# Taking the GpSimd relay out from between two convolution fills, and cutting the last store in three

## The chip, the cores and the metric

The kernel runs on one core of one Trainium2 chip. The metric is device microseconds of one execution. Beside it stands the span in the profile, from the first to the last instruction; in nearly every run here the time is 1.8 us above the span.

## The reference, cut to what matters

A causal convolution of width 7 per head over the sequence (8 heads of 24 channels, softmax-normalised weights), then a gated feed-forward layer.

```python
# x (8, 4096, 192); weight (8, 7); w_gate, w_val (192, 1536); w_out (1536, 192)
w    = softmax(weight, axis=-1)
conv = sum_k w[h, k] * x_padded[:, t + k, h]           # 32768 rows of 192
g    = conv @ w_gate
out  = (g * sigmoid(g) * (conv @ w_val)) @ w_out
```

## The kernel before

Rows are worked in 64 blocks of 512; two blocks (index `a` = 0 and 1) make a unit. TensorE convolves a unit with Toeplitz matrices in two *fills* of four heads. The result is evicted from PSUM into `stage`, transposed into `xq`, and goes through the gate, value and output matmuls. Unit 0 is transposed on TensorE; from unit 1 on `stage` goes through DRAM and comes back by three DMA transposes per block. Matmuls have 64 rows, so two run side by side as row tiles.

When two row tiles swap the PSUM banks that they write, the kernel puts in a *relay*: a GpSimd no-op that waits for the last matmul so far, and that the next such matmul waits for. The Trainium skill ("TensorEngine Tiling (Array Packing)", Gotcha 1: PSUM Pressure) gives the reason: row tiles cannot access the same PSUM bank at once, and software has to see to it. No run here tests that hazard.

```python
    def after_relay(mm):                     # called for conv and w_out matmuls
        last_mm[0] = mm
        if relay[0] is not None:
            tc.add_manual_dep(mm.ins, relay[0].ins.name, SYNC, ...)
            relay[0] = None

    def emit_relay():
        relay[0] = nc.gpsimd.nop(nofuse=True)
        tc.add_manual_dep(relay[0].ins, last_mm[0].ins.name, SYNC, ...)
    ...
    # head, in program order (cut)
    while first: emit_fetch(first)           # x of unit 0, GpSimd queue
    emit_busy(14)                            # filler matmuls that keep TensorE busy
    emit_gv_load(0); emit_gv_load(1); emit_wo_load(0); emit_gv_load(2)   # GpSimd queue
    ...                                      # Toeplitz matrices
    emit_busy(6)
    for fill in range(2):
        emit_conv(0, fill, spare=(fill == 1))      # fill 0 -> cps banks, fill 1 -> gate/val banks
        emit_relay()
        for a, mul in enumerate((nc.scalar.mul, nc.vector.tensor_scalar_mul)):
            emit_conv_out(0, fill, a, mul)         # ScalarE evicts block a=0, VectorE a=1
        if fill == 0:
            emit_dup(0, nc.vector.tensor_copy)
    first = fetches(1)                             # x of unit 1
    while first: emit_fetch(first)
    emit_wo_load(1)
    emit_busy(6)
    for b in range(UB):
        emit_pe_transpose_out(b, emit_pe_transpose(b))   # reads conv[0][rows, b, ...]
    emit_busy(4)
    # main loop: u is the unit, s the step in it; unit 1's conv at u = 0, s = 7 and 10,
    # DMA transposes of block 2 at s = 12..14; in between (cut):
            f0 = 14 if u == 0 else 0               # when unit u+2's x is loaded
    # last block's store
        if b == n_blocks - 1:
            nc.scalar.dma_start(out=o_v[:, 0:2], in_=o_sb[:, 0:2])
            return lambda: nc.sync.dma_start(out=o_v[:, 2:4], in_=o_sb[:, 2:4])
```

## Time and profile before

| | before |
|---|---|
| time, median of the first 3 runs | 813.46 us (812.72 to 813.50) |
| profiled run: time, span | 812.60, 810.8 us |
| TensorE busy | 802.2 us, 99% of the span |
| fill 0 / fill 1 of unit 0 begin | 8.66 / 10.49 us |
| first gate matmul | 13.73 us |
| last eviction ends, end of span | 807.05, 810.8 us |

From the profile's page (engine, busy us, share of the span and instructions; then the chain of waits by engine, POOL being GpSimd):

```profile
span 810.8 us, 30886 instructions
PE 802.2 (99%) x12884; PEld 507.5 (63%) x12884; DVE 558.5 (69%) x866; ACT 554.1 (68%) x967; POOL 133.6 (16%) x195
...
PE 98%; POOL 1%; issue 0%; DVE 0%; POOLq 0%
```

TensorE is the bound nearly everywhere. The 1% of GpSimd sits in the head. The chain of waits there, in order of time (start, us, what):

```profile
8.38 0.84 POOL wo_sb L145
9.22 0.62 POOL w_sb L139
9.83 0.60 POOL w_sb L140
10.44 0.01 POOLq L255
10.45 0.04 issue
10.49 0.24 PE gate L288
```

Fill 1 (`gate L288`) waited for the relay (L255), and the relay for GpSimd's issuing of weight loads, 0.6 to 0.84 us each. The same place in the timeline (start, us, engine, line, operation, output<-input; in brackets the idle time before it and what ended it; `cps`, `gate` and `val` are PSUM tiles):

```profile
9.32 0.57 ACT L304 ACTIVATE stage<-cps_198 128x480 f16<-128x480 f32 x1 [1.23 <-PE cps_199 L288]
9.36 0.66 DVE L304 TENSOR_SCALAR stage<-cps_199 128x480 f16<-128x480 f32 x1 [1.27 <-PE cps_199 L288]
10.12 0.47 DVE L312 COPY stage<-stage 128x640 f16<-128x640 f16 x1
10.49 0.24 PE L288 MATMUL gate<-x_0_82,toep 58*64 58x120 f16 x1 [1.21 <-POOLq L255]
11.14 0.57 ACT L304 ACTIVATE stage<-gate 128x480 f16<-128x480 f32 x1 [1.25 <-PE val L288]
11.18 0.66 DVE L304 TENSOR_SCALAR stage<-val 128x480 f16<-128x480 f32 x1 [0.59 <-PE val L288]
12.12 0.20 PE L346 MATMUL gate<-identity,stage 52*128 52x52 f16 x1
```

The reader is to see ScalarE (ACT), VectorE (DVE), and the transposes (L346). The tail, and below it the share and rate of the DMA engines in 40 slices of 0.11 us from 806.5 us on:

```profile
806.32 0.48 ACT L426 COPY o_sb<-acc_19289 128x384 f32<-128x384 f32 x1 [1.98 <-PE acc_19289 L414]
806.49 0.56 DVE L427 COPY o_sb<-acc_19290 128x384 f32<-128x384 f32 x1 [0.83 <-PE acc_19290 L414]
806.83 0.41 ACTq L430 DMA_DIRECT2D out_dram<-o_sb  x1
807.07 0.42 SPq L431 DMA_DIRECT2D out_dram<-o_sb  x1
```

```profile
DMA  0000000000059999999998400000000000000000
GB/s 0 0 0 0 0 0 0 0 0 0 0 123 294 375 348 321 314 308 328 328 328 301 130 0 0 0 0 0 0 0 0 0 0 0 0 0 0 0 0 0
```

Data moves for 1.3 us near 325 GB/s, then nothing for 1.9 us. For a DMA that GpSimd issues, the Trainium skill ("DMA: Bandwidth & Descriptors", Anatomy of one DMA) puts most of a fixed cost of about 2 us down to the receipt of the last write, heaviest for HBM. This store goes over the hardware queues of SP and ScalarE, which that section does not measure; the 1.9 us are of the same size.

### The profile page before, as it was taken

What the parts mean: (1) busy time and instruction counts of PE and PEld (TensorE: products, weight loads), DVE (VectorE), ACT (ScalarE), POOL (GpSimd) and SP (SyncE); (2) the same over time, 40 slices, a digit from 0 to 9 for tenths busy, and PEclk for the clock granted to TensorE, in tenths of its full rate; (3) what the DMA queues carried; (4) which work ended last, traced back from release to release, by engine and by line L of the source; (5) the groups of instructions that cost most, each with busy time, mean ns of one, the idle gap of its engine ahead of it and who ended that gap; (6) DMA issues with size and microseconds to landing.
All of it is one profiled execution on the core that took longest, in us unless ns stands there. A gap on an engine that the chain in (4) does not pass through costs nothing.

```text
span 810.8 us, 30886 instructions
## 1 busy us (share of the span) xinstructions
PE 802.2 (99%) x12884; PEld 507.5 (63%) x12884; DVE 558.5 (69%) x866; ACT 554.1 (68%) x967; POOL 133.6 (16%) x195
## 2 busy tenths in 40 slices
PE   7999999999999999999999999999999999999997
PEld 4666666666666666666666666666666666666665
DVE  6666667766667666677666767666776667676675
ACT  5677676667676776766777767767667677677664
POOL 6111111121111111111111111112111121111100
PEclk9999999999999999999999999999999999999999
DMA  9595654556554755546555556555555655464321
GB/s 136 94 143 99 117 96 97 124 97 112 117 90 108 131 98 110 95 99 122 110 109 108 84 115 130 99 104 105 99 119 104 119 104 92 107 130 92 92 75 40
DMA packets 187770, 85.53 MB, mean 105 GB/s; under 512 B 147678, under 2 KB 182590, under 8 KB 187630
## 3 DMA queue, kind: packets, MB, share of 16 engines
q0 software_dynamic: 52048, 42.26, 30.1%
q1 hardware_dynamic: 135310, 41.11, 24.3%
q8 instruction: 100, 1.64, 0.8%
q14 instruction: 40, 0.33, 0.1%
q10 hardware_dynamic: 272, 0.20, 0.1%
HBM read 34.95 MB, written 41.67 MB: 94 GB/s over the span
## 4 chain that ended last, share of the span: by engine, by line
PE 98%; POOL 1%; issue 0%; DVE 0%; POOLq 0%
PE gate L370 61%; PE val L370 1%; PE acc_763 L398 0%; PE acc_421 L398 0%; PE acc_420 L398 0%; PE acc_1702 L398 0%; PE acc_1363 L398 0%; PE acc_16113 L398 0%; PE acc_6505 L398 0%; PE acc_17314 L398 0%; PE acc_14912 L398 0%; PE acc_14575 L398 0%; PE acc_11310 L398 0%; PE acc_10971 L398 0%; PE acc_9772 L398 0%; PE acc_7706 L398 0%
## 5 line engine op out<-in xcount | busy, mean ns | idle before, releaser
L385 DVE TENSOR_TENSOR h<-sig,val 128x512 f16<-128x512 f16 x768 | 520.5, 688 | 242.8 <-PE val L370 240.9
L380 ACT ACTIVATE sig<-gate 128x512 f16<-128x512 f32 x768 | 458.5, 597 | 242.6 <-PE val L370 212.6
L370 PE MATMUL val<-xq,w_sb 64*128 64x512 f16 x2304 | 590.2, 376 | 0.0
L370 PE MATMUL gate<-xq,w_sb 64*128 64x512 f16 x2304 | 589.8, 376 | 0.0
L398 PEld LDWEIGHTS <-h 64*128 64x128 f16 x6120 | 268.2, 94 | 120.3
L370 PEld LDWEIGHTS <-w_sb 64*128 64x128 f16 x4608 | 212.7, 94 | 143.9 <-issue 1.2
L432 POOL DMA_DIRECT2D out_dram<-o_sb x63 | 48.5, 770 | 414.0 <-PE val L370 376.2
L288 PEld LDWEIGHTS <-toep 58*64 58x64 f16 x2048 | 29.4, 106 | 28.0 <-POOLq L255 14.1
L113 POOL DMA_DIRECT2D x_1_83<-in_x_dram x33 | 23.9, 724 | 94.2 <-PE val L370 79.7
L113 POOL DMA_DIRECT2D x_0_82<-in_x_dram x40 | 28.3, 709 | 61.9 <-PE val L370 49.5
L312 POOL COPY stage<-stage 128x640 f16<-128x640 f16 x31 | 22.3, 720 | 50.0 <-ACT sig L380 48.6
L98 POOL MEMSET x_0_82<- 6x192 f16 x8 | 2.0, 247 | 39.7 <-PE acc_8569 L398 6.1
L156 PE MATMUL busy<-idle 128*128 128x384 f16 x30 | 7.0, 386 | 0.0
L398 PE MATMUL acc_2301<-wo_sb,h 64*128 64x192 f16 x48 | 5.2, 243 | 0.0
L398 PE MATMUL acc_4104<-wo_sb,h 64*128 64x192 f16 x48 | 5.2, 243 | 0.0
L398 PE MATMUL acc_4968<-wo_sb,h 64*128 64x192 f16 x48 | 5.2, 243 | 0.0
L398 PE MATMUL acc_7706<-wo_sb,h 64*128 64x192 f16 x48 | 5.2, 243 | 0.0
L398 PE MATMUL acc_8570<-wo_sb,h 64*128 64x192 f16 x48 | 5.2, 243 | 0.0
L398 PE MATMUL acc_13712<-wo_sb,h 64*128 64x192 f16 x48 | 5.2, 243 | 0.0
L398 PE MATMUL acc_14576<-wo_sb,h 64*128 64x192 f16 x48 | 5.2, 243 | 0.0
L398 PE MATMUL acc_17314<-wo_sb,h 64*128 64x192 f16 x48 | 5.2, 243 | 0.0
L398 PE MATMUL acc_18180<-wo_sb,h 64*128 64x192 f16 x48 | 5.2, 243 | 0.0
(564 smaller groups left out, 871.3 us busy)
## 6 DMA issues: line engine op xcount, KB each, us to landing
out_dram<-o_sb POOLq DMA_DIRECT2D x63, 384.0 KB, 3.5
x_1_83<-in_x_dram POOLq DMA_DIRECT2D x31, 240.0 KB, 5.0
x_0_82<-in_x_dram POOLq DMA_DIRECT2D x24, 240.0 KB, 4.7
x_0_82<-in_x_dram POOLq DMA_DIRECT2D x8, 216.0 KB, 3.9
w_sb<-in_moe_w_gate_dram POOLq DMA_DIRECT2D x3, 192.0 KB, 5.3
wo_sb<-in_moe_w_out_dram POOLq DMA_DIRECT2D x2, 288.0 KB, 7.9
w_sb<-in_moe_w_val_dram POOLq DMA_DIRECT2D x3, 128.0 KB, 5.3
xc_639<-stage SPq DMA_DIRECT2D x2, 130.0 KB
```

The lines of the kernel that those rows point to most:

```text
L98: nc.gpsimd.memset(x16[0:pad, 0, :], 0.0)
L113: nc.gpsimd.dma_start(out=dst, in_=src)
L156: nc.tensor.matmul(busy, idle[:, 0:P], idle[:, 0 : UB * D], start=True, stop=True)
L288: mm = nc.tensor.matmul(conv["ps"][a][i * Q : (i + 1) * Q, :, e, :], toep[a * Q : a * Q + R, h, c, :], x16[a * Q : a * Q + R, i * CG : (i ...
L312: copy(conv[u][:, :, :, D:XD], conv[u][:, :, :, 0:Q])
L370: last_mm[0] = nc.tensor.matmul(ps, w_r[lo : lo + Q, q, ts(j, P)], xq[lo : lo + Q, q, :], start=(q == 0), stop=(q == NQ - 1),)
L380: nc.scalar.activation(sj, ps, AF.Silu)
L385: nc.vector.tensor_tensor(hj, sj, ps, op=ALU.mult)
L398: mm = nc.tensor.matmul(acc[a][:, i, :], hlist[j][lo : lo + Q, ts(2 * a + i, P)], wo_r[lo : lo + Q, j, :], start=(j == 0 and half == 0 and ...
L432: return lambda: nc.gpsimd.dma_start(out=o_v, in_=o_sb)
```

## The change

Its intent: fill 1 writes other banks than fill 0, with each row tile still on a bank of its own, so no relay is needed between them; and the last store is cut into three pieces over the two hardware queues. The line that goes stands in a loop, so the relay after fill 1 goes too; TensorE did not wait for that one.

```diff
         if b == n_blocks - 1:
-            nc.scalar.dma_start(out=o_v[:, 0:2], in_=o_sb[:, 0:2])
-            return lambda: nc.sync.dma_start(out=o_v[:, 2:4], in_=o_sb[:, 2:4])
+            nc.sync.dma_start(out=o_v[:, 0:2], in_=o_sb[:, 0:2])
+            nc.scalar.dma_start(out=o_v[:, 2], in_=o_sb[:, 2])
+            return lambda: nc.sync.dma_start(out=o_v[:, 3], in_=o_sb[:, 3])
...
     for fill in range(2):
         emit_conv(0, fill, spare=(fill == 1))
-        emit_relay()
         for a, mul in enumerate((nc.scalar.mul, nc.vector.tensor_scalar_mul)):
```

## The prediction

> **What bounds the kernel.** TensorE. The page gives PE busy 802.2 us of an 810.8 us span (99%); the chain of waits puts 98% on PE. What remains is a head (first gate matmul at 13.73 in the timeline) and a tail (last PE work ends 806.46, span 810.8). The change touches only these.
>
> **Head, before.** Conv fill 0 of unit 0 issues at 8.66 to 9.06 (timeline); fill 1 starts at 10.49. PE waits 1.2 us (its weight load 1.36), released by GpSimd's queue, not by data. The relay no-op sits in GpSimd's program behind nine weight-load issues, the last starting at 10.44: PE waits for GpSimd's issuing (0.54 to 0.86 us each), not for the hazard. Fill 1 uses other PSUM banks, whose readers finished before fill 0.
>
> **What removing it gives.** Fill 1 can start at about 9.1, 1.38 us sooner. Not all survives:
> - PE order alone (fill 1, six fillers, transposes) would put the transposes at 10.7 instead of 12.11.
> - They also need fill 1's evictions. VectorE evicts fill 0 from 9.36 to 10.02 (0.66), copies until 10.59 (0.47), and only then evicts fill 1 (0.66): done at 11.25. ScalarE is done at 10.5. So the transposes start at about 11.3: VectorE becomes the bound, the head gains 0.8 us, and PE idles about 0.5 us before them, less than the present 1.2 us gap that left the clock at 1.00.
> - PE did not wait for the second relay; without it GpSimd issues unit 1's x loads at about 11.0 instead of 11.72 (it idled 0.75).
> - Data: the first w_sb slice lands by 10.5, the last by 17.5, the first half of wo by 15.6, all in time. The second x load lands at 12.45+7.7 = 20.15; its conv starts at 20.75 and would start at 19.95. The DMA engines are full until about 19.5, so the earlier issue may not land much earlier: up to 0.2 us can be lost.
> Net head gain 0.6 to 0.8 us. PE is saturated afterwards, so it should carry to the end.
>
> **Tail.** The last store's data (two pieces of 192 KB, ACT issue 806.83, SP 807.07) moves from about 807.6 to 808.9 at 320 to 330 GB/s, all 16 engines 0.9 busy; then nothing moves until 810.8. The Trainium skill ("Trainium Kernel Development and Optimization", Key Constraints) says the SP, ACT and GpSimd queues share the same 16 engines, and issuing from several saves only issue time; this trace agrees in that two queues together stop at 330 GB/s. The change swaps queues and halves the second piece, issued at about 807.07 (ACT) and 807.25 (SP, after its first issue of 0.42). The first piece alone lasts until about 808.25 (estimate: 192 KB at 325 GB/s), which covers the later issue; bytes and copies are the same. Gain 0, within 0.2 us. The last 1.9 us stays.
>
> **Prediction.** 813.46 - 0.75 = 812.7 us; 8 in 10 within 811.9 to 813.4 (runs of before spread 0.8 us). Faster by over 2%: 0.005; within: 0.99; slower: 0.005.
>
> **To check.** Right: fill 1 at about 9.1, no GpSimd release of PE in the head; transposes at 11.3, released by VectorE's eviction; first gate matmul near 12.95; x loads issued near 11.0; last eviction to end 3.75 us as now. Wrong: PE waiting for x at unit 1's first conv, a low clock in the head, a tail changed by over 0.2 us, or the main loop's relay waits (14.1 us in 31) changed by the shift.

## The result, and the profile after

Four runs gave 811.34 to 811.48 and 811.14, median 811.38 us, against 813.17 for four runs of before. The ratio of the two is 0.9978 (95% interval 0.9961 to 0.9995). Ratios here are the mean time of one kernel's fast runs over that of the other's of the same rounds, so not quite the ratio of the medians. The prediction, 812.7 with a range of 811.9 to 813.4, missed: the time lies below the range.

The two profiled runs differ by less than the medians: 812.60 and 811.41 us, spans 810.8 and 809.6. The page's lines after:

```profile
span 809.6 us, 30885 instructions
PE 803.1 (99%) x12884; PEld 507.7 (63%) x12884; DVE 558.2 (69%) x866; ACT 554.3 (68%) x967; POOL 133.6 (17%) x195
...
PE 99%; DVE 1%; issue 0%; ACT 0%
```

GpSimd is gone from the chain. The head in the timeline:

```profile
8.73 0.88 PEld L288 LDWEIGHTS <-toep 58*64 58x64 f16 x64 [0.32 <-issue]
9.39 0.57 ACT L304 ACTIVATE stage<-cps 128x480 f16<-128x480 f32 x1 [1.23 <-PE cps L288]
9.43 0.66 DVE L304 TENSOR_SCALAR stage<-cps 128x480 f16<-128x480 f32 x1 [1.29 <-PE cps L288]
9.86 0.56 ACT L304 ACTIVATE stage<-gate 128x480 f16<-128x480 f32 x1
10.19 0.37 DVE L312 COPY stage<-stage 128x640 f16<-128x640 f16 x1
10.48 0.64 DVE L304 TENSOR_SCALAR stage<-val 128x480 f16<-128x480 f32 x1
10.78 0.19 PE L346 MATMUL gate<-identity,stage 52*128 52x52 f16 x1
12.41 0.82 PE L370 MATMUL gate<-xq,w_sb 64*128 64x512 f16 x3
```

The 64 weight loads of both fills are now one run. The transposes begin at 10.78, before VectorE has done fill 1 (10.48 + 0.64 = 11.12), and the first gate matmul at 12.41 instead of 13.73: 1.32 us sooner. Some of it is lost in unit 1's first conv, in the chain of waits:

```profile
19.50 0.78 PE cps L288 x32
```

It takes 0.78 us; the same step before ran from 20.82 to 21.36, 0.54. The second x load of unit 1, issued at 11.65, lands 8.0 us later, at 19.65: inside this conv. That costs 0.24 here; in other profiles with the same order of loads this wait was between 0 and 0.26 (e1, e7 and e11 0.55 us for the conv, e5 0.62, e12 0.80, e13 0.81). From block 1 to block 63 every last eviction lies 1.10 or 1.11 us earlier than before; the main loop takes the same 12.38 us per block in every profile once it is in step.

The tail:

```profile
805.21 0.48 ACT L426 COPY o_sb<-acc 128x384 f32<-128x384 f32 x1 [1.98 <-PE acc L414]
805.38 0.56 DVE L427 COPY o_sb<-acc 128x384 f32<-128x384 f32 x1 [0.83 <-PE acc L414]
805.72 0.42 SPq L430 DMA_DIRECT2D out_dram<-o_sb  x1
805.97 0.37 ACTq L431 DMA_DIRECT2D out_dram<-o_sb  x1
806.24 0.40 SPq L432 DMA_DIRECT2D out_dram<-o_sb  x1
```

From the end of the last eviction to the end of the span: 809.6 - 805.94 = 3.66 us, against 810.8 - 807.05 = 3.75 before. The span is given to 0.1 us, so this is no difference.

The sum of the profiles: 1.38 (the gap falls from 1.40 to 0.02) - 0.07 (fill 0 itself began later) - 0.24 (x) + 0.1 (tail, rounding) = 1.2 us, which is 810.8 - 809.6. The measured 1.79 is 0.6 more.

### The profile page after: what moved, and what is told of

It reads as the page before. It is cut to its first block, busy times and chain, and to the rows that moved or that the text cites. A ratio compares the mean times of both kernels' runs of the same rounds, so it can differ in the third digit from the quotient of the medians.

```text
span 809.6 us, 30885 instructions
## 1 busy us (share of the span) xinstructions
PE 803.1 (99%) x12884; PEld 507.7 (63%) x12884; DVE 558.2 (69%) x866; ACT 554.3 (68%) x967; POOL 133.6 (17%) x195
## 4 chain that ended last, share of the span: by engine, by line
PE 99%; DVE 1%; issue 0%; ACT 0%
PE gate L370 61%; PE acc L398 31%; PE cps L288 4%; PE val L370 1%; PE busy L156 0%; DVE band L222 0%; PE acc L414 0%; PE gate L346 0%; PE tps L232 0%; DVE o_sb L427 0%; DVE wn L213 0%; DVE toep L189 0%; DVE mask L193 0%; PE gate L288 0%; DVE shift L168 0%
## 5 line engine op out<-in xcount | busy, mean ns | idle before, releaser
L398 PE MATMUL acc<-wo_sb,h 64*128 64x192 f16 x6120 | 336.6, 243 | 0.0
L113 POOL DMA_DIRECT2D x<-in_x_dram x73 | 52.2, 716 | 155.3 <-PE val L370 129.4
L304 ACT ACTIVATE stage<-cps 128x480 f16<-128x480 f32 x125 | 71.0, 568 | 1.8 <-PE cps L288 1.6
L288 PE MATMUL cps<-x,toep 58*64 58x120 f16 x2016 | 38.9, 216 | 0.0
L427 DVE COPY o_sb<-acc 128x384 f32<-128x384 f32 x64 | 35.2, 550 | 0.8 <-PE acc L414 0.8
L426 ACT COPY o_sb<-acc 128x384 f32<-128x384 f32 x64 | 30.7, 480 | 2.0 <-PE acc L414 2.0
L98 POOL MEMSET x<- 6x192 f16 x8 | 2.0, 248 | 39.6 <-PE acc L398 39.6
L156 PEld LDWEIGHTS <-idle 128*128 128x128 f16 x30 | 3.2, 118 | 3.2 <-issue 2.4
L222 DVE COPY_PREDICATED band<-mask,whl 19x104 int32<-19x104 int32 x7 | 2.0, 279 | 0.2
```

The lines of the kernel that those rows point to most:

```text
L113: nc.gpsimd.dma_start(out=dst, in_=src)
L156: nc.tensor.matmul(busy, idle[:, 0:P], idle[:, 0 : UB * D], start=True, stop=True)
L288: mm = nc.tensor.matmul(conv["ps"][a][i * Q : (i + 1) * Q, :, e, :], toep[a * Q : a * Q + R, h, c, :], x16[a * Q : a * Q + R, i * CG : (i ...
L304: mul(conv[u][:, a, :, d0 : d0 + FH * grp], conv["ps"][a].rearrange("p g e d -> p g (e d)"), 1.0 / SCALE,)
L398: mm = nc.tensor.matmul(acc[a][:, i, :], hlist[j][lo : lo + Q, ts(2 * a + i, P)], wo_r[lo : lo + Q, j, :], start=(j == 0 and half == 0 and ...
L426: nc.scalar.copy(o_sb[:, 0:2, :], acc[0])
```

## The experiments

Eighteen experiments ran, some of them the same kernel again, in five groups (e1 to e4, e5 to e8, e9 to e12, e13 to e16, e17 and e18), each group on a chip of its own. All results were correct. Line numbers shift by a few where lines were added or removed. "Gap" is the time between the two fills: the start of fill 1 less the start of fill 0, less the 0.43 us in which the 32 matmuls of a fill start (before: 10.49 - 8.66 - 0.43 = 1.40). The idle time in brackets, 1.21, is shorter because it counts from the end of the last matmul.

### Each half of the change alone (e1, e2)

e1 takes out only the `emit_relay()` line; e2 has only the new store.

> The change without its store half: only the relay between and after the two conv fills of unit 0 is gone. Theory A (all of the gain is the head, and the store is worth nothing): time as the whole change, 811.2 to 811.6 us, runs within 0.4 us of each other; first gate matmul near 12.4 as in the after profile; last eviction to end 3.75. Theory B (the head gives the 1.1 us that the two profiles show and the store gives the other 0.6 to 0.7 of the measured 1.8): 812.0 to 812.2.

> The change without its head half: relay kept, last store in three pieces over the two queues. Theory A (store worth nothing): time as before, 812.7 to 813.5, with the same spread of 0.8 us between runs, if that spread comes from the head's wait for GpSimd's issuing. Theory B (store gives 0.6 to 0.7 us and removes the spread): 812.4 to 812.6 with a spread of 0.3 us or less. The profile tells the spread's place: fill 1's start near 10.5 in both, and last eviction to end 3.75 (A) or shorter (B).

| | profiled run | its gap | tail | all runs | ratio to before |
|---|---|---|---|---|---|
| e1 relay gone | 811.44 us | 0.01 us | 3.69 us | 811.44 to 814.35, median 812.32 | 0.9994 (0.9981 to 1.0008) |
| e2 new store | 812.73 | 1.11 | 3.66 | 812.03 to 814.56, median 812.64 | 0.9999 (0.9987 to 1.0012) |
| before, same chip | | | | 812.08 to 814.27, median 812.77 (11 runs) | |

The store alone gave nothing, and its tail is the tail of the others: theory B is out. The relay alone gave, in the profiled run, what the whole change gives; in the times of all runs its interval contains 1, so it is the trace that shows the gain. But both expectations on spread failed: five runs of e1 spread over 2.9 us. The profiles show one source. In e2, the first gates of block 2 wait for a DMA transpose (0.52 us in all, near 38 us), in e1 0.14; in the profiles of before and after there is no such wait. And in the gap of e2 is a second: 1.11 us instead of 1.40, depending on when GpSimd reaches the no-op. The no-op stands behind all nine weight loads in the program, yet it ran when the record of the last one began (before, 10.44), halfway through the last but one (e2, 10.13), or as that one began (e6 below, near 9.77). By what rule it gets past them is not shown.

### Which eviction do the transposes wait for? (e3)

```diff
-        for a, mul in enumerate((nc.scalar.mul, nc.vector.tensor_scalar_mul)):
+        muls = (nc.scalar.mul, nc.vector.tensor_scalar_mul)
+        for a, mul in enumerate(muls if fill == 0 else muls[::-1]):
```

> On top of the whole change: VectorE and ScalarE swap which half of fill 1 they evict, so the half of block 0 now comes last, from VectorE, at about 11.1. Theory A (block 0's transposes wait for block 0's eviction alone, so in the after kernel for ScalarE's, done at 10.4, and the fillers until 10.8 hide it): the transposes now start at 11.15 to 11.2 instead of 10.78 and the first gate matmul at 12.8, 0.4 later. In the time, up to 0.24 of that is hidden by the wait for unit 1's x at 19.6, so +0.15 to +0.4 us over the whole change. Rival (the transposes wait for neither eviction, only the fillers): no change at 10.78. Rival (they wait for both evictions, and VectorE was simply faster than predicted): no change, still 10.78 to 10.9.

```profile
9.76 0.56 ACT L304 ACTIVATE stage<-val 128x480 f16<-128x480 f32 x1
10.09 0.47 DVE L312 COPY stage<-stage 128x640 f16<-128x640 f16 x1
10.48 0.64 DVE L304 TENSOR_SCALAR stage<-gate 128x480 f16<-128x480 f32 x1
11.22 0.18 PE L346 MATMUL gate<-identity,stage 52*128 52x52 f16 x1 [0.47 <-issue]
12.84 0.39 PE L370 MATMUL gate<-xq,w_sb 64*128 64x512 f16 x1
```

VectorE ends at 11.12 as in the after profile, but now it evicts block 0 (`gate`), and the transposes begin at 11.22 instead of 10.78, the first gate at 12.84. The trace puts the wait down to "issue" and does not name VectorE; that it is VectorE's eviction follows from the edit, which changes nothing else, and from the time, 0.10 us after that eviction. Both rivals are out. These are nearly the times that the prediction gave for the change (11.3 and 12.95): it had the engine right and the block wrong. The conv of unit 1 then began at 19.86, after x had landed, and took 0.55, so part of the loss was hidden: the profiled span is 809.8, 0.2 above after's (median of four 811.95).

### Unit 1's x loaded earlier (e4)

```diff
     emit_wo_load(0)
+    first = fetches(1) if n_units > 1 else []
+    while first:
+        emit_fetch(first)
     emit_gv_load(2)
...
-    first = fetches(1) if n_units > 1 else []
-    while first:
-        emit_fetch(first)
     emit_wo_load(1)
```

> On top of the whole change: unit 1's two x loads issue before the last three weight loads instead of after them. Theory A (the after kernel loses 0.24 us in unit 1's first conv, 32 matmuls in 0.78 instead of 0.54, because the second x load lands at 19.65): the conv takes 0.54 again and the time is 0.2 to 0.3 us below the whole change, 811.0 to 811.2, if the last weight slice still lands before its use near 19.98. Rival (the conv is slow for another reason, such as its weight loads): still 0.78, no gain. If the last slice lands late, a wait moves to the gate matmul near 20 and the gain is lost.

```profile
19.39 0.54 PE cps L291 x32
```

The conv takes 0.54 again, so the 0.24 was the wait for x. One profile would not be enough here, since e1, e7 and e11 have 0.55 without this edit; but all six profiles with x this early (e4, e8, e10, e15, e16, e18) have 0.54 or 0.55, and those with the old order of loads range up to 0.81. Yet the time did not fall: 811.39 us median (811.08 to 811.92), profile 809.6 like after's. In the timeline:

```profile
36.54 0.38 PE L373 MATMUL gate<-xq,w_sb 64*128 64x512 f16 x1
...
37.09 0.37 PE L373 MATMUL gate<-xq,w_sb 64*128 64x512 f16 x1 [0.17 <-DMA xq<-xc]
```

The third gate matmul of block 2 comes 0.55 us after the second instead of 0.21, released by the DMA transpose. What was won at 19 us was given back at 37.

### Does the competition with unit 2's x make the transposes late? (e5 to e8)

e5 is the change unaltered. e6 (before), e7 (after) and e8 (e4) load unit 2's x in the head, after the second `wo` load at 13 us, instead of at step 14 near 29 us:

```diff
     emit_wo_load(1)
+    first = fetches(2)
+    while first:
+        emit_fetch(first)
     emit_busy(6)
...
-            f0 = 14 if u == 0 else 0
-            if u + 2 < n_units:
+            f0 = 0
+            if u > 0 and u + 2 < n_units:
```

> The whole change, unaltered, on the chip of the next three runs, to have its spread beside theirs. Theory C (the time of one run depends on when block 2's three DMA transposes land, which compete with unit 2's x loads; a late landing makes the first gates of block 2 wait, as 0.50 us in e2, 0.14 in e1, 0.33 in e4): runs spread by 0.5 us or more, lowest near 811.1. Theory D (the spread before the change came from PE's wait for GpSimd in the relay, which the change removed): 811.1 to 811.5, spread 0.4 or less.

> The kernel before, with unit 2's x loads issued in the head (after the second wo load, some 13 us) instead of in the middle of block 2's transposes (about 29 us). Theory C: the transposes land well before their use, the spread falls from 2.2 us to 0.5 or less and the time to 812.0 to 812.5, below the 812.77 of before; no wait for a transpose in the profile. Theory D: the spread stays at 1 to 2 us, since the relay stays.

> The whole change with unit 2's x loads issued in the head. Theory C: 811.0 to 811.4 with a spread of 0.4 or less; and against e6, with the transposes out of the way on both sides, the change is worth the head's gain that the profiles show and no more: 1.0 to 1.3 us (1.4 of the relay gap less 0.24 for unit 1's x). Theory D: same as e5.

> Both: unit 1's x before the last weight loads (as e4) and unit 2's x in the head. In e4 the 0.24 us won in unit 1's first conv (block 0's eviction came 0.35 us sooner than in the after profile) was lost again where block 2 waited for its third transpose (0.33). Theory C: here it stays, so 0.2 to 0.35 us below e7: 810.7 to 811.1. If e4's loss had another cause, it is lost again and the time equals e7.

| | profiled span | all runs, us |
|---|---|---|
| before, same chip | | 811.85 to 813.38, median 812.92 (9 runs) |
| e5 after | 813.6 | 815.38, 813.09, 811.18, 811.36, 813.07 |
| e6 before, x of unit 2 early | 810.3 | 812.12, 811.70, 812.62, 812.23, 812.19 |
| e7 after, x of unit 2 early | 809.3 | 811.06, 811.34, 812.52, 811.60, 812.43 |
| e8 both x early | 809.3 | 811.06, 811.39, 811.09, 813.10, 811.06 |

e5's profiled run is the slow one, and shows where its 4 us went. First the timeline, then busy times in two stretches (stretch; length; busy us and instructions of PE, PEld, DVE, ACT, POOL; granted clock; DMA share; GB/s):

```profile
37.02 0.37 PE L370 MATMUL gate<-xq,w_sb 64*128 64x512 f16 x1
...
39.47 0.37 PE L370 MATMUL gate<-xq,w_sb 64*128 64x512 f16 x1 [2.06 <-DMA xq<-xc]
...
40.42 0.63 PE L370 MATMUL gate<-xq,w_sb 64*128 64x512 f16 x1
```

```profile
39.40:41.60 2.20, 2.13 (x20) 1.22 (x19) 0.69 (x1) 0.60 (x1) 0.25 (x1) 0.62 0.02 7
41.60:43.50 1.90, 1.90 (x40) 1.08 (x40) 0.69 (x1) 1.17 (x2) 0.47 (x1) 0.55 0.52 79
```

The third transpose came so late that TensorE stood still for 2.06 us (2.45 from gate to gate, 0.21 being usual). Then its clock was granted at 0.62 and 0.55 for 4 us. Between block 0 and block 1 this run lost 4.1 us: 2.5 in two late gates (0.50 and 2.45 us after the gate before, instead of 0.21 each) and the other 1.6 at the low clock.

With unit 2's x out of the way, no profile (e6 to e8) shows a wait for a transpose any more. The step from block 0's last eviction to block 1's, 12.38 us without such a wait, is 12.37 to 12.39 in all seven profiles that load unit 2's x early (e6 to e8, e10, e15, e16, e18); of the thirteen others, six are longer by 0.07 to 4.1 us. In e7 the DMA engines pause between the transposes (30.4 to 30.9 and 31.6 to 32.2 us), where in the after profile they are busy without a pause to speak of from 29.7 to nearly 36. The profiled spans of e6 and e7, with no transpose wait on either side, differ by 1.0 us, of which the gap is 0.73 (the gap of e6's own profile) and the wait for x in e6 0.24. The spread of before fell from 1.5 to 0.9 us and its median by 0.7. But the expected 0.5 or less was met by none, and e8 still had a run at 813.10. So theory C explains the one run near 815 that was traced, and a part of the rest; something else adds 1.7 us to some runs. Theory D, that the change removes the spread, fell with e5, whose ratio to before is 0.9994 (0.9980 to 1.0007). e8 was to lie 0.2 to 0.35 us below e7 and its profile equals e7's: in e7 the conv of unit 1 happened not to wait for x (0.55 us), so there was nothing left to win.

### The relay left in, with GpSimd's loads behind it; and other checks (e9 to e12)

e9 is the kernel before, with its relays, and with the last weight loads moved:

```diff
     emit_wo_load(0)
-    emit_gv_load(2)
...
         if fill == 0:
             emit_dup(0, nc.vector.tensor_copy)
+    emit_gv_load(2)
     first = fetches(1) if n_units > 1 else []
```

> The kernel before, relays kept, with the last three weight loads issued after the two fills instead of before them. Theory E (the gap costs what GpSimd's program order costs, not what the hazard costs): the relay no-op now follows seven weight-side issues, the last dispatched near 8.3, so fill 1 starts 0.1 to 0.2 us after fill 0's last matmul (about 9.2 to 9.3) with the relay still there, and the first gate matmul comes at 12.4 to 12.5, like the whole change. Rival F (the relay's round trip PE to GpSimd to PE costs most of the 1.4 us): the gap stays 0.7 us or more. The last weight slice is issued after a second relay, near 9.9, and must land before its use near 20; if it lands late a wait appears there.

```profile
9.43 0.46 PEld L287 LDWEIGHTS <-toep 58*64 58x64 f16 x32 [0.30 <-POOLq L254]
```

The gap shrinks from 1.40 to 0.33 us with the relay still there. So some 0.3 us are the relay's own round trip (more than the 0.1 to 0.2 expected), and the other 1.1 were GpSimd's program order; rival F is out. The last load before the no-op, the first `wo` load, was issued from 8.33 to 9.19, so no load was still to be started when fill 0 ended. The first gate comes at 12.67 (12.4 to 12.5 was expected) and five runs lie at 811.71 to 812.36 (median 812.00; before on that chip 812.26 to 813.48, median 812.55).

e10 is e8 with block 0's store issued at step 22 instead of 17:

```diff
-        if s % NCH == 5 and stores or not live:
+        if (g == 22 if u == 0 else s % NCH == 5) and stores or not live:
```

> e8 with block 0's store, which competes with block 2's transposes for the DMA engines, issued five steps later (near 36 us instead of 31.5). Theory C2 (what is left of the spread in e7 and e8, one run at 813.1, is still late transposes): all five runs at 811.0 to 811.4. Rival (what is left comes from elsewhere, for example the head's weight loads): a spread of over 0.5 us stays in some runs and no transpose wait shows.

Its runs: 811.39, 813.12, 812.99, 811.05, 811.65. No x load and no store competes with the transposes any more, and two of five runs are near 813.1: what theory C2 forecast did not come, though the two slow runs themselves left no trace. The profiled run, 811.39, shows a smaller source:

```profile
10.09 0.68 DVE L315 COPY stage<-stage 128x640 f16<-128x640 f16 x1
11.39 0.20 PE L349 MATMUL gate<-identity,stage 52*128 52x52 f16 x1 [0.16 <-DVE stage L307]
```

VectorE's copy between its two evictions took 0.68 us, so its eviction of block 1 ended at 11.33, and block 1's transposes waited for it: they began 0.71 us after block 0's instead of 0.39. The same kernel in e15 had a copy of 0.33, no such wait, and took 811.08. In e5, e11 and e12 (copy 0.47) the same wait cost 0.1 us. What lengthens the copy is not shown.

e11 puts all three pieces of the last store on the SP queue (`nc.sync` for `nc.scalar` in the second).

> The whole change with all three pieces of the last store on the one SP queue. If the tail is bound by the bytes at 320 to 330 GB/s and by the fixed time after the last byte, as the prediction has it: last eviction to end 3.65 to 3.8, as with two queues. If two queues help: 3.9 to 4.2, as the third issue then starts some 0.4 us later.

Last eviction to end: 809.5 - 805.71 = 3.79 us. Its third piece was issued 0.45 us later than in the after profile (0.75 instead of 0.30 us past the end of the last eviction) and the rate dipped to 164 GB/s in one slice of 0.11 us, but at most 0.1 us came of it. The tail is bound by bytes and by the 1.9 us after them; how many queues issue it hardly matters.

e12 is the change a third time.

> The whole change again, as the measure for e9 and e10 on their chip, and for the spread: if the first four runs (811.14 to 811.48) were lucky, some of these five lie above 811.7, up to 815, and the lowest is again 811.1 to 811.4.

811.44, 811.11, 811.43, 811.88, 815.77, 813.08: ratio to before 1.0000 (0.9983 to 1.0016). As expected, the first four runs were lucky.

### Catching a slow run in a profile (e13 to e16)

Four profiled looks, two at the change and two at e10's kernel.

> One more profiled look at the whole change, to catch one of its slow runs (813.07, 813.08 and 813.09 so far, some 1.7 us above its usual 811.1 to 811.5) in a trace. If it is slow: theory C3 says a wait of PE for a transpose of block 2 of 0.5 us or more, near 36 to 38 us; theory G says matmuls of twice the usual start-to-start time for some 3 us (the granted clock halved) without such a wait before them. If it is fast it says only that the usual head is 12.3 to 12.5.

> As the run before: a slow run shows either the late transpose (C3) or a stretch of half clock without one (G).

> A look at the kernel of e10, two of whose five runs took 812.99 and 813.12, although its transposes compete with no x load and no store. If it is slow: C3 says a late transpose all the same, G a stretch of half clock without one, and a third possibility is a late weight or x load before 30 us (a gap at the first use of a weight slice near 16.6 or 20, or at unit 1's conv near 19.4).

> As the run before: a slow run shows a late transpose (C3), a stretch of half clock (G), or a late load in the head.

e13, e15 and e16 were fast (811.36, 811.08, 811.18). e14 took 813.19. Its fill 0, as matmuls with their shortest, median and longest time in ns and their first and last start, and the stretch of both fills in the view of stretches:

```profile
L288 PE MATMUL cps<-x,toep x32: 302/304/307, 9.9 to 10.6; 58*64 58x120 f16 x32
```

```profile
9.90:11.60 1.70, 1.70 (x66) 1.58 (x66) 0.57 (x1) 0.57 (x1) 1.70 (x3) 1.00 1.25 183
```

The same line of the after profile:

```profile
L288 PE MATMUL cps<-x,toep x32: 212/213/237, 8.7 to 9.1; 58*64 58x120 f16 x32
```

In e14 TensorE works at half pace until about 11.3 us: the fillers follow each other by 0.32 us, each fill takes 0.80 to 0.85 us instead of 0.44, and only near the end of fill 1 the matmuls shorten from 0.30 to 0.21. Fill 0 begins 1.2 us later than in the after profile, the first gate 1.86 us later (14.27), and from block 1 on the run is 1.75 us behind. A late transpose cost it 0.12 us at most. In the fast profiles the matmuls went to full pace between about 5.2 us (e2) and 7.6 us (e1); in the after profile at about 7.4, just before fill 0, and its fill 0 began at 8.73 instead of 8.63 as in most. The granted clock reads 1.00 through this stretch: that column does not show it, the matmuls' own durations do.

The Trainium skill ("TensorE: Matmul & The Clock Gate", Part 1: The HAM clock gate) describes this: TensorE starts at half clock and is released by a window of sustained activity, about 3.4 us long, that runs free of the kernel, so that the moment varies from run to run. e14 looks like this, though no record of the clock in its trace says so; the size does not fit: here half pace lasted 8.9 us from the first filler (2.39).

### Starting the fillers earlier (e17, e18)

```diff
+    emit_busy(3)
     nc.tensor.matmul(wbc, ones, wraw, start=True, stop=True)
     emit_busy(14)
```

> The whole change with three more filler matmuls in front of the first real one, so TensorE is busy from about 1.2 us instead of 2.4 while it waits for the first load. The profile of e14 (813.19) shows fillers 0.32 to 0.35 us apart until about 10 us and both fills in 0.80 and 0.85 us instead of 0.44, so half rate until then; fast profiles go to full rate between 5 and 7 us. Theory G (the slow runs near 813.1 are runs whose clock rises late, and it rises a set time after activity begins): it rises about 1.2 us sooner, so no run lies between 812.8 and 813.4; fast runs stay at 811.1 to 811.5. Rival (the moment does not depend on when TensorE begins): one or two of five runs still near 813.1. A run near 815 would be a late transpose as in e5.

> The kernel of e10 with the same three early fillers. Theory G: neither the late clock nor late loads are left, so all five runs lie at 811.0 to 811.5, against two of five near 813.1 in e10. Rival: one or two near 813.1 again.

e17 (the change with early fillers): 811.47, 811.94, 811.46, 811.39, 811.55. e18 (e10's kernel with them): 811.39, 811.46, 811.39, 812.40, 811.39; the 812.40 has a span of 809.7, like the others, so its excess lies outside the instructions. None of ten runs is near 813.1, against 4 of 17 of the change and 3 of 12 of e8 and e10's kernel. If the rate had stayed at a quarter, ten without one would happen about once in eighteen times (0.75 to the tenth is 0.06), so this supports theory G and does not prove it; besides, all ten ran on one chip on which the unaltered change did not run, so that chip itself is a rival that was not tested. Nor do the two profiles show the clock rising sooner than in other fast ones (full pace near 6 us); what is seen is only that in none of ten runs it rose late. It costs something: the three fillers push the first real matmul back and fill 0 begins at 8.96 instead of 8.63, so the best runs are 811.39 instead of 811.1. By its mean, 811.56, e17 was still well below the change's seventeen runs (below), on another chip. No single version here is proven faster than the change by its interval; e17's ratio to before is 0.9988 (0.9975 to 1.0002).

## Why the prediction was wrong

All seventeen runs of the changed kernel: ten at 811.11 to 811.48, one at 811.88, four at 813.07 to 813.19, two above 815; median 811.44, mean 812.28. All 45 runs of before: 811.85 to 814.64, median 812.72, mean 812.81. So the change is worth 1.3 us by the medians, 0.5 by the means over all chips, and 1.8 in the four runs that it was first measured by. Only those four have an interval without 1; e5's and e12's contain it. That the head is shorter, the traces show; how much of it the time keeps on average, these runs do not settle.

- **"Fill 1 can start at about 9.1, 1.38 us sooner": right.** It began at 9.18, the gap fell to 0.02 us, and the relay waited for GpSimd's issuing, as e9 shows. That the gap is itself a matter of chance was missed: 1.40, 1.11 and 0.73 us in three profiles with the relay and the loads before it.
- **"They also need fill 1's evictions. VectorE ... done at 11.25 ... So the transposes start at about 11.3: VectorE becomes the bound, the head gains 0.8 us": wrong; this is the step that failed.** The 30 transposes that come first read block 0, which ScalarE evicts and had done at 10.42. They began at 10.78, behind the fillers, which is the 10.7 that the prediction itself gives for "PE order alone", and VectorE's half was there at 11.12, about when block 1's transposes came up (11.18). The head gained 1.32 us, not 0.8. e3 shows it: with the two engines swapped the transposes begin at 11.22. VectorE does bound block 1's transposes, but by 0 to 0.1 us in most profiles and 0.3 in e10.
- **"Up to 0.2 us can be lost" on unit 1's x: right in kind**, 0.24 in this profile, 0 in three others of the same order; e4 takes it away.
- **"PE is saturated afterwards, so it should carry to the end": right for the profile, wrong as a rule.** Between block 0 and block 1 stands another deadline, block 2's DMA transposes. In e4 it took back 0.33 us, in e5 4.1.
- **"Gain 0, within 0.2 us" for the tail: right.** 3.66 to 3.79 us in every profile where it was read, with either store and with one queue.
- **The range: wrong.** Its lower end, 811.9, held a net head gain of at most 0.8 us and a spread taken from three runs. With the right head gain the same sum is 1.32 - 0.24 = 1.1 us, so about 812.4 from the median of 813.46, and still not 811.38. The rest, 0.6 us, is which runs were met: the medians of 4 runs compare a before whose profiled run was 0.6 us faster than its median (812.60 and 813.17) with an after of which all four runs were of its fast kind. What made each of the timed runs fast or slow is not on record, as only profiled runs leave a trace; that the causes found (GpSimd's pace in the gap, x of unit 1, VectorE's copy, late transposes, a late clock) are all of it is not shown.

That a late clock hurts the changed kernel more than the kernel before, whose TensorE stood waiting for part of that time anyway, would explain why the means differ by only 0.5. That is argued; no slow run of before was traced.

## What to carry to other kernels

A semaphore relayed through an engine that also issues DMAs can cost what stands before it in that engine's program (here 0.4 to 1.1 us on top of 0.33): look in the chain of waits at what the relay itself waited for, and move either one. When a stage gets a head start, ask for each consumer which half of which buffer it reads before naming the new bound, and which later deadline (a load, a transpose) the earlier work will run into. When an expected gain is 0.1% of the time, read it in two traces, step by step; four runs may all be of one kind.

## What the Trainium skill lacked or had wrong

- "TensorE: Matmul & The Clock Gate" (Part 1, and Why this matters for your kernels) gives some 3.4 to 4 us of activity until full clock, give or take 0.5. Counted from the first filler at 2.4 us, the fast profiles here show full pace after about 3 us (e2) to 5 us (e1, after), and e14 after 8.9 us, which cost 1.75 us, although TensorE was busy almost without a pause.
- The same page warns of idle gaps over about 3 us. In e5 a gap of 2.06 us was followed by 4 us at a granted clock of 0.62 and 0.55.
- The same page (Part 1) warns that the trace's records of the clock gate have been seen to be unreliable. It does not say what was seen here, that the profile's granted clock can read 1.00 while matmuls run at half pace (e14: a fill in 0.80 us instead of 0.44, its matmuls 302 ns long instead of 212).
- "DMA: Bandwidth & Descriptors" calls the descriptor generation of a GpSimd DMA small and the time to initiate a DMA usually small relative to the DMA itself. That holds here (0.54 to 0.86 us of issue per weight load, medians of 4.5 to 7.8 us to landing in the after profile). What it lacks is that such issues add up for other work of the same engine: a no-op behind them held TensorE for up to 1.40 us.
- No page gives the price of a relay from TensorE over GpSimd and back: 0.33 us in e9, with no load still to be started in front of it.
- The page on DMA gives a bandwidth for DMA transposes but, as far as I found, no time to landing for one beside other traffic. Here one that TensorE waited for lay some 7.6 us in the chain of waits (e4 and e2), and PE's wait for it ranged from none to 2.06 us between runs of the same program.
